# Five seven-product groups instead of three in FFN1, on eight single PSUM banks, with a new order of steps

## The chip, the cores and the metric

The kernel runs on one core of a Trainium2 chip. Times are device microseconds (us) of that core; "span" is the time from the first to the last instruction in a profiled execution, 1.7 to 2.4 us less than the timed value. Engines: PE is the matrix engine (TensorE), PEld its weight load, DVE VectorE, ACT ScalarE, POOL GpSimd, SP SyncE. PSUM is where the kernel has PE put its products, in eight banks; its other tiles lie in SBUF.

## The reference

```python
scores = np.matmul(q, k.transpose(0, 1, 3, 2)) / np.sqrt(64)   # q, k, v: (8, 8, 576, 64)
scores = np.where(np.abs(pos[:, None] - pos[None, :]) <= 32, scores, -1e9)
x = softmax(scores) @ v                       # -> tokens: (4608, 512)
g, val = x @ w_gate, x @ w_val                # w: (512, 1536)       "FFN1"
out = (g * sigmoid(g) * val) @ w_out          # w_out: (1536, 512)   "FFN2"
```

## The kernel before

The 4608 tokens are nine chunks of 512. Attention for the next chunk is woven into FFN2 of the present one. From chunk 1 on, products of 2 x 2 blocks are done with seven block products instead of eight (a Winograd form of Strassen's scheme), which costs sums of blocks on DVE and POOL. In FFN1 three groups use it; six hidden tiles are plain "units". FFN2 uses it for everything.

```python
PSUM: ps_a 2 double banks, ps_c 1 double bank, ps_o 2 single banks, open for the whole kernel

def ffn1_grouped(j):
    load_v(j + 1, range(5))                      # POOL's DMA queue
    xs = x_sums(j, nc.gpsimd)                    # four sums of xT, 128x512, on POOL (DVE in chunk 1)
    ...                                          # carried pairs: AV, norm, DMA transpose x -> xT
    # (cut) three groups of P1..P7, six units, q/k loads q0..k4 on POOL's queue between them
    # FFN2 sums: As = wino_sums(j, 0, 1, nc.gpsimd), Ds = wino_sums(j, 1, 2, nc.gpsimd),
    #            Bs = wino_sums(j, 2, 5)         # DVE, three groups wide: 128x768

def wino_sums(j, lo, hi, eng=None):
    tt = lambda o, a, b, op: (eng or nc.vector).tensor_tensor(out=o, in0=a, in1=b, op=op)
    return [lambda: tt(s1, a21, a22, ALU.add), lambda: tt(s2, s1, a11, ALU.subtract),
            lambda: tt(s3, a11, a21, ALU.subtract), lambda: tt(s4, a12, s2, ALU.subtract)]

def pair_xt(m):  nc.sync.dma_start_transpose(out=dst, in_=x16[0])      # x -> xT, SP's queue
def pair_mask(m): nc.vector.tensor_tensor(out=flat, in0=flat, in1=mask, op=ALU.mult)
```

Of the kernel before, what the change touches and what calls it, by code (L numbers as in the profile page):

```python
# [132 lines left out]
def kernel(  # L133
# [29 lines left out]
    qk16 = fast.enter_context(tc.tile_pool(name="qk16", bufs=4))  # L163
    tkpool = fast.enter_context(tc.tile_pool(name="tk", bufs=18))
# [6 lines left out]
    ps_a = fast.enter_context(tc.tile_pool(name="ps_a", bufs=2, space=bass.MemoryType.PSUM))  # L171
    ps_c = fast.enter_context(tc.tile_pool(name="ps_c", bufs=1, space=bass.MemoryType.PSUM))
    ps_o = fast.enter_context(tc.tile_pool(name="ps_o", bufs=2, space=bass.MemoryType.PSUM))
# [102 lines left out]

    def cast_qk(st, cast):
        t16 = qk16.tile([128, J9, 2, D], FP16, tag="qk16", name="t16")
        cast(t16.rearrange("p j h d -> p h j d"),
             st.rearrange("p h (j d) -> p h j d", d=D))  # L280
        return t16
# [56 lines left out]
    def quad_scores(ms, F):  # L338

        if ms not in quads:  # L340
            quads[ms] = ppool.tile([128, 2, 2, 2, HP, 64], FP16, tag="p2", name="p2_t", bufs=2)
            for n, m in enumerate(ms):
                pts[m] = quads[ms][:, n]
# [56 lines left out]
    def turn_x(ms, pool, cast=None):  # L400
# [15 lines left out]
        cast(dst.rearrange("p g (n t) -> p n g t", t=128), tp)  # L416
# [38 lines left out]
    def group_weights():  # L455

        s3 = qkst.tile([128, 3, 2, 768], FP16, tag="qkst", name="g_top")
        s4 = const.tile([128, 2, 768], FP16, name="g_rest")
        half = lambda w, k: w[:, 2 * k:2 * k + 2].rearrange(
            "p k (a c) -> p k a c", c=512)[:, :, :, 0:256]  # L460
        v0, v1, g0, g1 = half(wv16, 0), half(wv16, 1), half(wg16, 0), half(wg16, 1)
        gw["s"] = [s3[:, 0], s3[:, 1], s3[:, 2], s4]
        t1, t2, t3, t4 = [t.rearrange("p k (a c) -> p k a c", c=256) for t in gw["s"]]
        return [lambda k=k, o=o, a=a, b=b, op=op:
                nc.vector.tensor_tensor(out=o[:, k], in0=a[:, k], in1=b[:, k], op=op)
                for o, a, b, op in ((t1, g0, g1, ALU.add), (t2, t1, v0, ALU.subtract),
                                    (t3, v0, g0, ALU.subtract), (t4, v1, t2, ALU.subtract))
                for k in range(2)]

    def group_steps(j, i, xs, tiles):  # L470

        f = 2 * i
        x = xts[j]
        b11, b21, b22 = x[:, 0:2, 0:256], x[:, 2:4, 0:256], x[:, 2:4, 256:512]
        wv = lambda k: wv16[:, 2 * k:2 * k + 2, 512 * i:512 * i + 256]
        wg = lambda k: wg16[:, 2 * k:2 * k + 2, 512 * i:512 * i + 256]
        s1, s2, s3, s4 = [t[:, :, 256 * i:256 * i + 256] for t in gw["s"]]
        k = {}
        first = "ZX" if i == 2 else "X"

        def product(name, lhs, rhs, first):
            for n in range(2):
                for g in range(2):
                    nc.tensor.matmul(out=k[name][:, n], lhsT=lhs[:, g, 128 * n:128 * n + 128],  # L484
                                     rhs=rhs[:, g, :], start=(first and n == 0 and g == 0),
                                     stop=(g == 1), skip_group_check=True)

        def bank(name):
            pool = tiles[name]
            t = pool.tile([128, 2, 256], FP32, tag="c" if pool is ps_c else "o",  # L490
                          name=f"g{name}_ps")
            k[name] = t

        def keep_act(name, src):
            k[name] = opool.tile([128, 2, 256], FP32, tag="kept", name="kept", bufs=3)
            cast_act(k[name], k[src])

        def val(c, src, name):
            if "val" not in k:
                k["val"] = qk16.tile([128, 2, 512], FP16, tag="qk16", name="val")  # L500
            nc.vector.tensor_tensor(out=k["val"][:, :, 256 * c:256 * c + 256], in0=k[src],  # L501
                                    in1=k[name], op=ALU.add)
# [5 lines left out]
        def silu(c, src):  # L508
            if "silu" not in k:
                k["silu"] = qk16.tile([128, 2, 512], FP16, tag="qk16", name="silu")  # L510
            nc.scalar.activation(out=k["silu"][:, :, 256 * c:256 * c + 256], in_=k[src],  # L511
                                 func=AF.Silu, bias=0.0, scale=1.0)

        return {
            "P1": lambda: ([bank(n) for n in first], product("X", wv(0), b11, True)),
            "s1": lambda: keep_act("s1", "X"),
            "P2": lambda: (bank("Y"), product("Y", wv(1), b21, True)),
            "c11": lambda: val(0, "Y", "s1"),
            "P5": lambda: ("Z" in k or bank("Z"), product("Z", s1, xs[0], True)),
            "p5": lambda: keep_act("p5", "Z"),  # L520
            "P6": lambda: product("X", s2, xs[1], False),
            "u2": lambda: keep_act("u2", "X"),
            "P7": lambda: product("X", s3, xs[2], False),
            "c22": gate,
            "sc": lambda: silu(1, "gate"),
            "P3": lambda: product("Z", s4, b22, False),
            "c12": lambda: val(1, "Z", "u2"),
            "P4": lambda: product("X", wg(1), xs[3], False),
            "sd": lambda: silu(0, "X"),
            "hm": lambda: nc.vector.tensor_tensor(out=hts[j][:, 2 * f:2 * f + 2, :],  # L530
                                                  in0=k["silu"], in1=k["val"], op=ALU.mult),
        }

    def x_sums(j, eng):

        x = xts[j]
        b11, b12 = x[:, 0:2, 0:256], x[:, 0:2, 256:512]
        b21, b22 = x[:, 2:4, 0:256], x[:, 2:4, 256:512]
        t = ppool.tile([128, 4, 2, 256], FP16, tag="p2", name="x_sums", bufs=2)
        t1, t2, t3, t4 = [t[:, n] for n in range(4)]  # L540
        for o, a, b in ((t1, b12, b11), (t2, b22, t1), (t3, b22, b12), (t4, b21, t2)):
            eng.tensor_tensor(out=o, in0=a, in1=b, op=ALU.subtract)  # L542
        return t1, t2, t3, t4

    def unit_steps(j, fk):
# [3 lines left out]
        def half(i, w, parts=None):  # L549
            if i == 0:  # L550
                k["gv"] = ps_a.tile([128, 2, 512], FP32, tag="a", name="gv_ps")
            for g, c in parts or [(g, slice(0, 512)) for g in range(GS)]:
                nc.tensor.matmul(out=k["gv"][:, i, c], lhsT=w[:, g, 128 * fk:128 * fk + 128],  # L553
                                 rhs=xts[j][:, g, c], start=(g == 0 and c.start == 0),
                                 stop=(g == GS - 1), skip_group_check=True)

        def silu():
            k["s"] = spool.tile([128, 512], FP16, tag="s", name="ssb")
            nc.scalar.activation(out=k["s"], in_=k["gv"][:, 0, :], func=AF.Silu, bias=0.0,  # L559
                                 scale=1.0)  # L560

        first, second = [(0, slice(0, 256))], [(0, slice(256, 512))]
        most = [(g, slice(0, 512)) for g in range(1, GS)]
        return {"pg": lambda: half(0, wg16), "pv": lambda: half(1, wv16), "s": silu,
                "pva": lambda: half(1, wv16, first), "pvb": lambda: half(1, wv16, second),
                "pvm": lambda: half(1, wv16, most), "pvn": lambda: half(1, wv16, most + second),
                "m": lambda: nc.vector.tensor_tensor(out=hts[j][:, fk, :], in0=k["s"],  # L567
                                                     in1=k["gv"][:, 1, :], op=ALU.mult)}
# [3 lines left out]
    def wino_weights():  # L572
# [3 lines left out]
        rest = qkst.tile([128, 2, FKS // 2, 256], FP16, tag="qkst", name="ws_rest")  # L576
# [12 lines left out]
    def wino_sums(j, lo, hi, eng=None):  # L589

        h = hts[j].rearrange("p (f c) q -> p f c q", c=2)[:, lo:hi]
        a11, a21 = h[:, :, 0, 0:256], h[:, :, 0, 256:512]
        a12, a22 = h[:, :, 1, 0:256], h[:, :, 1, 256:512]
        s1, s2, s3, s4 = [t[:, lo:hi] for t in ws["s"]]
        tt = lambda o, a, b, op: (eng or nc.vector).tensor_tensor(out=o, in0=a, in1=b, op=op)  # L595
        return [lambda: tt(s1, a21, a22, ALU.add), lambda: tt(s2, s1, a11, ALU.subtract),
                lambda: tt(s3, a11, a21, ALU.subtract), lambda: tt(s4, a12, s2, ALU.subtract)]

    def wino_steps(j, split):
# [24 lines left out]
        def product(dst, lhs, rhs, first):  # L624
            for n in range(2):
                for f in range(FKS // 2):
                    nc.tensor.matmul(out=dst[n], lhsT=lhs[:, f, 128 * n:128 * n + 128],  # L627
                                     rhs=rhs[:, f, :],
                                     start=(first and f == 0 and (split or n == 0)),
                                     stop=(f == FKS // 2 - 1), skip_group_check=True)  # L630

        def keep_act(name, src):
            t = opool.tile([128, 2, 256], FP32, tag="kept", name="kept", bufs=3)
# [13 lines left out]
        def total(src, name, i, c, put=True):  # L647
# [13 lines left out]
            "p1": lambda: product(x, a(0, 0), b11, True),  # L661
            "s1": lambda: keep_act("s1", x),
            "p2": lambda: product(y, a(0, 1), b21, True),
            "c11": lambda: total(y, "s1", 0, 0),
            "p6": lambda: product(x, s2, t2, False),
            "u2": lambda: keep_act("u2", x),
# [326 lines left out]
```

## Time and profile before

| | before |
|---|---|
| time, median of 3 runs | 321.18 us (319.95 to 323.24) |
| span of the profiled run, granted clock | 317.8 us, 0.993 |
| chunks 1 to 8, start to start (the last to PE's end) | 32.07, 32.50, 32.00, 32.28, 31.77, 32.30, 29.30, 29.41 us |
| waits of PE with a named releaser after 59 us, summed | 0.6 us |

The prediction below reads the page, the stretches and PE's timeline (columns: start, time, engine, line, operation, tiles, how many, and in brackets the idle time before). In the timeline of VectorE in chunk 2's FFN2 (columns: start, time, engine, line, operation, tiles, how many, and in brackets the idle time before) a wide and a narrow sum together take 0.75 us, three masks 1.88 us.

```profile
113.17 0.75 DVE L595 TENSOR_TENSOR s_top<-hT 128x768 f16<-128x768 f16 x2
...
115.68 1.88 DVE L322 TENSOR_TENSOR p_t<-p_t,mask 128x1024 f16<-128x1024 f16 x3
```

POOL's timeline of the same place: it has only DMA issues there, until the new chunk's token sums. Those wait for xT, and stand in the queue in front of the q/k loads (tok).

```profile
110.78 2.67 POOL L242 DMA_DIRECT2D v<-in_v_dram  x3
...
123.15 1.53 POOL L542 TENSOR_TENSOR x_sums<-xT 128x512 f16<-128x512 f16 x1 [4.12 <-DVE xT L271]
...
128.08 0.92 POOL L223 DMA_DIRECT2D tok<-in_q_dram  x1
```

### The profile page before, as it was taken

The numbers are of one execution on the slowest core, as the hardware profiler recorded it, in microseconds if no ns is written. First come the engines' busy times: TensorE is split into PE (matmuls) and PEld (weight loads), VectorE is DVE, ScalarE is ACT, GpSimd is POOL, SyncE is SP. The second block draws the span as 40 slices with busy tenths as digits, with TensorE's granted clock in tenths as the row PEclk, the third lists the DMA queues.
The fourth block names the chain that finished last, engine by engine and source line by source line (L and its number), as shares of the span: only waits on it lengthen the run. The fifth ranks groups of instructions, "written<-read, shape, count | busy, mean of one in ns | idle before, by whom it ended". The sixth has DMA issues, their size and how long they took to land.

```text
span 317.8 us, 8145 instructions
## 1 busy us (share of the span) xinstructions
PE 303.6 (96%) x3220; PEld 213.2 (67%) x3220; DVE 219.1 (69%) x404; ACT 192.7 (61%) x309; POOL 182.4 (57%) x231
## 2 busy tenths in 40 slices
PE   5779999999999999999999999999999999999991
PEld 3444555676877687768776877677767776777581
DVE  2654398788866787678757885887588958737760
ACT  3774559665756575667466846684668566336530
POOL 8973678649358934994489339953440538303300
PEclk9999999999999999999999999999999999999997
DMA  7999999999959996999799989999651330030012
GB/s 274 166 192 296 244 179 177 200 143 165 158 136 128 172 163 142 121 183 152 164 132 161 159 171 124 136 175 163 153 127 42 95 92 3 24 110 0 0 51 92
DMA packets 155916, 44.22 MB, mean 139 GB/s; under 512 B 136416, under 2 KB 153312, under 8 KB 155872
## 3 DMA queue, kind: packets, MB, share of 16 engines
q0 software_dynamic: 100640, 16.52, 79.3%
q1 hardware_dynamic: 55232, 27.11, 40.7%
q8 instruction: 27, 0.44, 0.6%
q14 instruction: 17, 0.14, 0.2%
HBM read 37.75 MB, written 9.44 MB: 148 GB/s over the span
## 4 chain that ended last, share of the span: by engine, by line
PE 88%; DVE 4%; DMA 3%; ACT 2%; issue 1%; SPq 0%; ACTq 0%
PE gv_ps L553 26%; PE gX_ps L484 13%; PE x_ps L627 12%; PE y_ps L627 9%; PE gZ_ps L484 7%; PE gv_ps L427 6%; PE o_ps L374 4%; PE gY_ps L484 3%; PE ob L441 3%; PE s_ps L312 3%; DMA qk_st<-in_k_dram 3%; PE xt_ps L414 1%; DVE s_top L595 1%; PE z_ps L627 1%; DVE p_t L358 1%
## 5 line engine op out<-in xcount | busy, mean ns | idle before, releaser
L553 PE MATMUL gv_ps<-xT,wv 128*128 128x512 f16 (+1 forms) x224 | 57.2, 349 | 0.0
L553 PE MATMUL gv_ps<-xT,wg 128*128 128x512 f16 x192 | 49.4, 379 | 0.0
L542 POOL TENSOR_TENSOR x_sums<-xT 128x512 f16<-128x512 f16 x14 | 17.4, 1246 | 49.1 <-DVE xT L271 29.3
L595 POOL TENSOR_TENSOR s_top<-hT 128x256 f16<-128x256 f16 x32 | 21.6, 674 | 40.1 <-PE gY_ps L484 28.8
L318 ACT ACTIVATE p_t<-s_ps 128x1024 f16<-128x1024 f32 (+1 forms) x40 | 34.7, 924 | 14.2 <-PE s_ps L312 14.2
L268 ACT ACTIVATE kept<-gX_ps 128x512 f32<-128x512 f32 x48 | 28.6, 595 | 18.1 <-PE gX_ps L484 18.1
L567 DVE TENSOR_TENSOR hT<-ssb,gv_ps 128x512 f16<-128x512 f16 x48 | 32.7, 682 | 9.9 <-ACT ssb L559 9.9
L559 ACT ACTIVATE ssb<-gv_ps 128x512 f16<-128x512 f32 x48 | 28.6, 596 | 17.1 <-PE gv_ps L553 17.1
L506 DVE TENSOR_TENSOR gate<-gX_ps,kept 128x512 f32<-128x512 f32 x24 | 16.6, 692 | 25.9 <-PE gX_ps L484 17.0
L553 PEld LDWEIGHTS <-wv 128*128 128x128 f16 x224 | 21.9, 98 | 17.9
L484 PEld LDWEIGHTS <-g_top 128*128 128x128 f16 x288 | 27.5, 98 | 6.6 <-ACT kept L268 1.5
L627 PEld LDWEIGHTS <-hT 128*128 128x128 f16 x288 | 27.4, 98 | 5.3 <-issue 0.3
L627 PEld LDWEIGHTS <-s_top 128*128 128x128 f16 x288 | 27.7, 98 | 4.1 <-issue 0.6
L511 ACT ACTIVATE silu<-gate 128x512 f16<-128x512 f32 x24 | 15.1, 630 | 24.5 <-DVE gate L506 24.5
L484 PE MATMUL gX_ps<-x_sums,g_top 128*128 128x256 f16 x192 | 28.8, 273 | 0.0
L553 PEld LDWEIGHTS <-wg 128*128 128x128 f16 x192 | 17.6, 98 | 14.6
L501 DVE TENSOR_TENSOR val<-gY_ps,kept 128x512 f16<-128x512 f32 x24 | 16.5, 687 | 14.8 <-ACT kept L268 13.6
L223 POOL DMA_DIRECT2D tok<-in_q_dram x30 | 25.8, 860 | 1.1 <-DMA wo<-in_moe_w_out_dram 1.1
L223 POOL DMA_DIRECT2D tok<-in_k_dram x30 | 25.9, 862 | 0.5 <-DMA wo<-in_moe_w_out_dram 0.5
L392 DVE TENSOR_TENSOR x<-o_ps,rall 128x512 f16<-128x512 f32 x36 | 24.9, 691 | 1.2
L627 PE MATMUL x_ps<-w_top,s_top 128*128 128x256 f16 x192 | 23.6, 273 | 0.0
L322 DVE TENSOR_TENSOR p_t<-p_t,mask 128x1024 f16<-128x1024 f16 x32 | 21.4, 705 | 1.8 <-ACT p_t L318 1.1
(114 smaller groups left out, 618.4 us busy)
## 6 DMA issues: line engine op xcount, KB each, us to landing
out_dram<-osb SPq DMA_DIRECT2D x32, 256.0 KB, 3.1
v<-v SPq DMA_DIRECT2D x12, 264.0 KB, 5.7
v<-in_v_dram POOLq DMA_DIRECT2D x24, 128.0 KB, 7.1
tok<-in_q_dram POOLq DMA_DIRECT2D x24, 128.0 KB, 6.3
tok<-in_k_dram POOLq DMA_DIRECT2D x24, 128.0 KB, 6.5
qk_st<-in_q_dram SPq DMA_DIRECT2D x4, 576.0 KB, 6.9
qk_st<-in_k_dram SPq DMA_DIRECT2D x4, 576.0 KB, 9.1
v<-in_v_dram POOLq DMA_DIRECT2D x16, 96.0 KB, 6.7
```

Of the source, the lines that this page charges most:

```text
L223: nc.gpsimd.dma_start(out=t[0:n].rearrange("p (h d) -> p h d", d=D), in_=src[b].rearrange("h s d -> s h d")[128 * m:128 * m + n])
L268: nc.scalar.activation(out=o, in_=i, func=AF.Copy, bias=0.0, scale=1.0)
L318: nc.scalar.activation(out=o, in_=s, func=AF.Exp, bias=0.0, scale=1.0 / float(D) ** 0.5)
L322: nc.vector.tensor_tensor(out=flat, in0=flat, in1=mask, op=ALU.mult)
L392: nc.vector.tensor_tensor(out=x16s[m][:, a], in0=ov[:, :, :, 0:D], in1=r.unsqueeze(3).to_broadcast([128, a.stop - a.start, 4, D]), op=ALU. ...
L427: nc.tensor.matmul(out=gv[:, i, :], lhsT=w[:, g, 128 * fk:128 * fk + 128], rhs=xts[j][:, g, :], start=(g == 0), stop=(g == GS - 1))
L484: nc.tensor.matmul(out=k[name][:, n], lhsT=lhs[:, g, 128 * n:128 * n + 128], rhs=rhs[:, g, :], start=(first and n == 0 and g == 0), stop=( ...
L553: nc.tensor.matmul(out=k["gv"][:, i, c], lhsT=w[:, g, 128 * fk:128 * fk + 128], rhs=xts[j][:, g, c], start=(g == 0 and c.start == 0), stop ...
L559: nc.scalar.activation(out=k["s"], in_=k["gv"][:, 0, :], func=AF.Silu, bias=0.0, scale=1.0)
L567: "m": lambda: nc.vector.tensor_tensor(out=hts[j][:, fk, :], in0=k["s"], in1=k["gv"][:, 1, :], op=ALU.mult)}
L595: tt = lambda o, a, b, op: (eng or nc.vector).tensor_tensor(out=o, in0=a, in1=b, op=op)
L627: nc.tensor.matmul(out=dst[n], lhsT=lhs[:, f, 128 * n:128 * n + 128], rhs=rhs[:, f, :], start=(first and f == 0 and (split or n == 0)), st ...
```

## The change

Its intent: five of six hidden-tile pairs go through the seven-product scheme instead of three, so FFN1 needs fewer matmul columns. To interleave five groups, PSUM is closed and reopened as eight single banks for FFN1 and as the old pools for FFN2. The order of all steps is written out anew, with a bank behind `@` and an engine behind `/` (D is DVE, G is POOL). FFN2's sums are single 256-wide instructions now, 24 a chunk, spread over DVE and POOL, partly within FFN2.

```diff
+    def open_psum(*pools):
+        psum.close()
+        return [psum.enter_context(tc.tile_pool(name=n, bufs=b, space=bass.MemoryType.PSUM,
+                                                reuse_waits="tile")) for n, b in pools]
 ... (cut: chunk 0 builds the weight sums of five groups, 16 instructions, from unit 4 on)
-    def wino_sums(j, lo, hi, eng=None):          # one sum over several groups
+    def wino_sum(j, p, n, eng):                  # one sum of one group p
 ...
-    ORDER = """ pg0 pva0 pvm0 q0 k0 q1 t0 1P1 1s1 ... """
+        "even": """ (start and FFN1 cut) ... 4sd 4h0 u51m
+            4h1 S30/D tabE S40/D sc0@4@5 sc12@0@1@2@3 S50/D S51/D S02/G S41/D F1a@6 ex0 ex2 ld3 F1
+            S01/D Fs1 F2@7 S12/G S10/G k2 S11/G ex1 S31/G k0 F6 k1 S52/G Fc11 S33/D av012@4@5@0@1@2@3
+            S22/D m1 S42/G m0 F5 Fu2 F7 S13/G Fk5 sc34@4@5@0@1 m2 ex4 xtp@2@3 S43/D ex3 S53/D S03/G
+            Fc22 tabS xtc/D k4 F3 F4 Fc12 Fc21 k3 """
+        for token in ORDER[name].split():
+            if stage == 0 and banks and step[:3] != "av" and step[:3] != "u50":
+                single = open_psum(*[(f"ps_{i}", 1) for i in range(8)])
+            elif stage == 1 and step in ("sc0", "sc12", "F1a"):
+                ps_a, ps_c, ps_o = open_psum(*PAIRED)
```

In that order S30 is the first sum of group 3, F6 the FFN2 product that reads all sums S·1 (which are built from S·0), k a softmax mask, m a normalisation, av012 the attention products of three pairs, T1 to T4 the token sums. A carried pair is an attention pair left over from the chunk before.

## The prediction

> **What bounds the kernel now.** I read the page first: the busy shares and the chain of work that ended last.
>
> ```profile
> PE 303.6 (96%) x3220; PEld 213.2 (67%) x3220; DVE 219.1 (69%) x404; ACT 192.7 (61%) x309; POOL 182.4 (57%) x231
> ...
> PE 88%; DVE 4%; DMA 3%; ACT 2%; issue 1%; SPq 0%; ACTq 0%
> ```
>
> The matrix engine carries 88% of the chain. I then cut the span at the first matmul of each chunk and asked for busy time by stretch; four of the stretches are these (chunks 1, 3, 7, 8).
>
> ```profile
> 59.70:91.78 32.08, 32.08 (x359) 23.74 (x358) 27.34 (x52) 20.53 (x34) 16.42 (x22) 1.00 1.70 151
> ...
> 124.28:156.29 32.01, 32.01 (x358) 23.70 (x358) 23.95 (x44) 20.22 (x34) 22.41 (x28) 1.00 1.58 148
> ...
> 252.64:282.04 29.40, 28.98 (x222) 21.37 (x222) 19.04 (x34) 13.53 (x25) 13.27 (x15) 1.00 0.18 54
> 282.04:317.80 35.76, 29.20 (x222) 21.13 (x220) 18.60 (x38) 15.29 (x30) 5.51 (x8) 0.94 0.14 47
> ```
>
> Columns are the stretch, its length, then busy time of PE, weight load, DVE, ACT and POOL, granted clock, DMA. PE is busy for the whole of chunks 1 and 3; only chunks 7 and 8 (0.4 us, and the 6 us tail) show idle time. Busy is not the same as at peak, so I looked at start-to-start times in PE's timeline of chunk 3.
>
> ```profile
> 130.20 0.60 PE L484 MATMUL gX_ps<-x_sums,wg 128*128 128x256 f16 x4
> 130.63 0.60 PE L484 MATMUL gX_ps<-xT,wv 128*128 128x256 f16 x4
> 131.07 0.27 PE L553 MATMUL gv_ps<-xT,wv 128*128 128x256 f16 x1
> ...
> 142.04 1.03 PE L553 MATMUL gv_ps<-xT,wg 128*128 128x512 f16 x4
> 142.91 1.03 PE L553 MATMUL gv_ps<-xT,wv 128*128 128x512 f16 x4
> 143.77 1.47 PE L627 MATMUL x_ps<-wo,hT 128*128 128x256 f16 x12
> ```
>
> Four 256-column matmuls take 0.437 us (130.20 to 131.07 is eight), so 109.3 ns each; eight 512-column ones take 1.73 us, so 216 ns each. These leave no slack: FFN1 of a chunk is a packed stream of columns, and only fewer columns or fewer matmuls make it shorter.
>
> **What the Trainium skill says.** "TensorE: Matmul & The Clock Gate", section "Wait — 56ns, not 53.3ns?", gives N/2.4 GHz plus about 2.5 ns start to start, 109.2 and 215.8 ns here: the trace agrees (109.3, 216). The same page, "What's actually happening", says an idle window of about 3.4 us halves PE's clock until a busy window has passed; before has no such gap in its middle and a clock of 1.00 there, so this case does not show it yet. "SBUF — State Buffer", "Who interferes with whom", says a DVE instruction with two SBUF inputs and a GpSimd instruction that reads SBUF exclude each other. The trace fits: the DVE product of silu and val (both SBUF) averages 822 ns in chunk 3 and 682 in chunk 1, where POOL meets it less. "PSUM — Partial Sum Buffer", "PSUM bank collisions raise a hardware error", says two engines must not be in one bank at once. So product P6, which adds into the bank that s1 is copied from, has to wait for ACT; the trace shows the weight load of such a product waiting 0.21 us for the copy in chunk 8.
>
> **The change part by part.** *Matmul columns.* Before, FFN1 of a chunk has three groups of 7 x 4 = 84 matmuls of 256 columns and six plain units: 42 matmuls of 512 columns and six split ones, 12 of 256. That is 96 x 109.3 + 42 x 216 ns = 10.49 + 9.07 = 19.57 us (trace, 124.28 to 143.93: 19.65). After, five groups are 140 matmuls of 256 and two units 16 of 512: 15.30 + 3.46 = 18.76 us. Saved: 0.81 us a chunk, **6.5 us** over eight. FFN2 keeps 84 matmuls, only reordered (F1a does ten of the first twelve, so it can start before the last pair). Scores, AV and transposes keep their number.
>
> *Evictions.* A group costs more outside PE. Spacing of back-to-back instructions in chunk 8's timeline gives the real price:
>
> ```profile
> 285.17 0.60 ACT L268 ACTIVATE kept<-gZ_ps 128x512 f32<-128x512 f32 x1 [0.39 <-PE gZ_ps L484]
> ...
> 285.67 0.59 ACT L268 ACTIVATE kept<-gX_ps 128x512 f32<-128x512 f32 x1
> ...
> 287.02 0.69 DVE L506 TENSOR_TENSOR gate<-gX_ps,kept 128x512 f32<-128x512 f32 x1
> ...
> 287.62 0.68 DVE L501 TENSOR_TENSOR val<-gZ_ps,kept 128x512 f16<-128x512 f32 x1
> ```
>
> 0.50 us for an ACT copy, 0.60 for a DVE op from PSUM. Narrow f16 sums on DVE start 0.21 apart, one of 512 elements about 0.34, a softmax normalisation 0.75. DVE in the new FFN1: ten val and five gate 9.0, products 4 x 0.60 + 2 x 0.33 = 3.1, two unit products 1.2, four token sums 1.4, early FFN2 sums 0.6, carried norms 0.8 to 1.5: about 16.4 of 18.8 us, 87%. Before: nine 5.4, three 1.8, six 3.6, sums about 2.3, norm 0.8: 13.9 of 19.65, 71%. ACT: 15 copies 7.5, ten silu 5.2, two unit silu 1.0: 13.7, 73%. A group asks DVE for 2.4 us and ACT for 2.5 while PE spends 3.06 on it, so neither becomes the bound on average, and the interleaving over eight banks puts two or three other products (0.9 to 1.3 us) between P1 and P6, about what a copy and its hand-over need. I allow **+1.0 us** in all for small bank waits, collisions with POOL's 12 to 15 sums a chunk, and the two reopenings of the pools, and take off **0.3** for the gaps in chunks 7 and 8.
>
> *Chunk 0.* Here I expect most of the saving to go. The group weights are now computed from unit 4 on instead of unit 8, in 16 DVE instructions instead of 8. The top one takes the fourth slot of the four-buffer staging pool; its last tenant is the fourth q/k tile of batch 1, free only when POOL has cast it. POOL's timeline, then DVE's, then PE's:
>
> ```profile
> 33.91 1.15 POOL L274 CAST t<-qk_st 128x1152 f16<-128x1152 f32 x1 [1.44 <-DMA qk_st<-in_q_dram]
> 36.53 1.15 POOL L274 CAST t<-qk_st 128x1152 f16<-128x1152 f32 x1 [1.48 <-DMA qk_st<-in_k_dram]
> ```
>
> ```profile
> 31.30 0.69 DVE L434 TENSOR_TENSOR hT<-ssb,gv_ps 128x512 f16<-128x512 f16 x1 [1.04 <-ACT ssb L433]
> 33.52 0.69 DVE L434 TENSOR_TENSOR hT<-ssb,gv_ps 128x512 f16<-128x512 f16 x1 [1.54 <-ACT ssb L433]
> ...
> 39.81 1.02 DVE L465 TENSOR_TENSOR g_top<-wg 128x768 f16<-128x768 f16 x2
> ```
>
> ```profile
> 34.42 0.67 PE L287 MATMUL qk_ps<-ident,t 128*128 128x128 f16 x9
> 34.92 1.03 PE L427 MATMUL gv_ps<-xT,wg 128*128 128x512 f16 x4
> ```
>
> That cast waits for a DMA and ends at 36.53 + 1.15 = 37.68. Before, the first group sum came at 39.81, after it. Now it stands right behind unit 4's product (31.30), so DVE, in order, is blocked from 32.0 to 37.7. Then two sums (1.0) and unit 5's product (0.69) run to about 39.5. PE has two double-bank buffers for units: unit 6 still goes, unit 7 (34.92 before) must wait for unit 5's buffer, so PE starts again near 39.5. That is **+4.6 us**, and nothing behind it has slack to take it back, since PE is packed to the end of chunk 7. A 4.6 us idle gap is longer than the skill's 3.4 us window; a whole free-running window falls inside with chance (4.6 - 3.4) / 3.4, about a third (an estimate from that page), costing some 1.7 to 3 us: **+0.7** on average.
>
> Sum: 321.2 - 6.5 - 0.3 + 1.0 + 4.6 + 0.7 = 320.7.
>
> **The rivals.** (1) *The clean saving*: the staging slot is free in time or the wait is not drawn. Then 321.2 - 6.5 - 0.3 + 1.0 = 315.4, 1.8% faster. For it: whoever chose unit 4 may have looked at the result. Against it: the DMA-bound cast at 36.5, which nothing in the change moves earlier. I give it 15%. (2) *DVE becomes the bound in FFN1*: with 87% average load and in-order waits on ACT, POOL and PE, bank releases come late and PE stalls 0.5 to 1 us a chunk, 4 to 8 us in all: 324 to 327 with the chunk 0 stall. For it: POOL lengthens DVE's products, and DVE carries two more groups. Against it: eight banks let PE run two to three groups ahead, and DVE has over 2 us of slack a chunk; 12%. (3) *DMA*: the mean busy share is in the nineties until 230 us, so chunks shorter by 2.5% could meet late q/k loads. Against: a load lands 6.5 us after issue and is needed a chunk later. I count nothing for it.
>
> **Range and chances.** Weighing the main case (320.7) against rival 1 below it and rival 2 above it, I put 320.0, with 315.8 to 323.0 for 8 in 10. Over 2% faster (below 314.8) needs rival 1 and hardly any bank wait: 0.06. Over 2% slower (above 327.6) needs rival 2 at its worst and the clock loss: 0.03. Within 2%: 0.91.
>
> **What would show it.** Right: chunk 0's PE timeline has a gap of 4 to 5 us before unit 7, released by DVE, and DVE's first group sum starts at about 37.7 after waiting for POOL's cast; chunks 1 to 6 are 31.2 to 31.6 us long; FFN1's matmuls keep 109.3 and 216 ns. Wrong: no such gap and chunks 1 to 6 below 31.4 us (rival 1); chunks still at 32 us or more with PE waiting on DVE's val, gate or sums (rival 2); a granted clock below 1 between 39 and 46 us would price the throttle.

## More of the kernel before

POOL does its eight sums of FFN2 (two of six groups) while FFN1 runs; FFN2 itself has none of its sums on POOL.

The view of the tile xT between 110 and 138 us gives, from issue to landing of its DMA transposes:

```profile
DMA to landing us min/median/max: 2.4/2.6/3.2
```

## The result, and the profile after

The changed kernel takes 350.25 us in the median of four runs (347.86 to 353.17) against 321.28 us (319.95 to 323.24) of the kernel before. The ratio is 1.087, with a 95% interval of 1.077 to 1.098: slower, and outside the predicted range. Ratios here are the mean time of one kernel's runs over that of the other's of the same rounds, so not quite the ratio of the medians. Executions over 1.5% slower than the fastest of the same kernel are left out of the means.

On the page, PE's busy time is what it was (303.6 us before), but its share of the span has fallen from 96% to 88%. The chain of work breaks off after 2% of the span in this trace, so it couldn't be used; the stretches and the timeline took its place.

```profile
PE 304.5 (88%) x3380; PEld 230.9 (67%) x3380; DVE 266.8 (77%) x497; ACT 217.0 (63%) x357; POOL 190.8 (55%) x250
...
PE 2%; DVE 0%; ACT 0%; issue 0%
```

The stretches of chunks 2 (up to its last FFN2 matmul, with the wait in front) and 3:

```profile
92.60:130.70 38.10, 33.74 (x394) 26.37 (x392) 29.86 (x56) 24.19 (x39) 25.36 (x32) 0.96 1.37 131
134.12:167.19 33.07, 31.87 (x392) 26.17 (x393) 28.94 (x54) 23.01 (x38) 19.36 (x25) 1.00 1.12 131
```

Before, PE was busy for all of chunk 3; now 1.2 us of it are idle, and 4.4 us of the chunk 2 stretch, where the clock is 0.96 too. PE's timeline says what it waits for. The lines are, in turn: unit 7 of chunk 0; FFN1 of chunk 1; an attention product in chunk 1's FFN2; the start of chunk 2 (three lines); product F6 in chunk 2; the starts of chunks 3 and 4.

```profile
34.44 1.03 PE L441 MATMUL gv_ps<-xT,wg 128*128 128x512 f16 x4
...
61.26 0.60 PE L509 MATMUL gZ_ps<-x_sums,g_top 128*128 128x256 f16 x4
61.70 0.60 PE L509 MATMUL gY_ps<-xT,wv 128*128 128x256 f16 x4
...
85.20 0.96 PE L385 MATMUL o_ps<-v,p_t 128*64 128x66 f16 x48 [1.70 <-DVE p_t L331]
...
95.34 1.03 PE L583 MATMUL gv_ps<-xT,wv 128*128 128x512 f16 x2 [2.57 <-DMA xT<-x]
96.17 1.91 PE L583 MATMUL gv_ps<-xT,wg 128*128 128x512 f16 x4
97.88 0.79 PE L583 MATMUL gv_ps<-xT,wv 128*128 128x512 f16 x2
...
121.33 1.49 PE L654 MATMUL x_ps<-w_top,s_top 128*128 128x256 f16 x12 [1.43 <-DVE s_top L624]
...
134.12 1.02 PE L583 MATMUL gv_ps<-xT,wv 128*128 128x512 f16 x4 [3.34 <-DMA xT<-x]
...
171.10 1.03 PE L509 MATMUL gX_ps<-xT,wv 128*128 128x256 f16 x8 [1.65 <-DVE hT L594]
```

FFN1 is as dense as predicted: groups of four matmuls start 0.44 us apart (61.26 and 61.70). The rest of the view is three kinds of wait. Summed over chunks 1 to 8 (start to start, less the plain time of the matmuls between, only where the trace names a releaser):

| PE waits for | where | sum |
|---|---|---|
| a late DVE result (sums, masks, hT, output sums) | FFN2 of all chunks | 16.5 us |
| the DMA transpose x to xT | start of chunks 2, 3, 5: 2.73, 3.50, 3.32 | 9.6 us |
| a PSUM bank at the reopening | start of chunks 4, 5, 6, 8: 1.71, 1.07, 1.69, 1.63 | 6.1 us |
| ACT | chunk 8 | 0.5 us |

That is 32.6 us (before rounding) against 0.6 us before. With the 6.5 us of saved columns, a start of chunk 1 that is 1.0 us earlier, and two spells of slow clock of 1.5 us each (behind the wait at 95 us eight matmuls take 3.25 us from 95.34 to 98.59, 1.73 at 216 ns; behind a wait of 2.44 us in chunk 7 24 matmuls take 4.09 us from 303.42 to 307.51, 2.62 at 109.3 ns), the balance is 32.6 - 0.6 - 6.5 - 1.0 + 3.0 = 27.5 us. The spans differ by 346.2 - 317.8 = 28.4 us. The 0.9 us left are small gaps without a releaser; some are matmuls whose records are missing.

Why two waits slowed the clock and others, longer ones, did not can be read from the stretches. In each trace the changes of clock lie on a grid of 3.41 us. Four stretches of that grid in after (PE's busy time stands behind the comma, the clock third from the end):

```profile
91.43:94.84 3.41, 1.34 (x13) 0.95 (x10) 1.29 (x2) 1.33 (x3) 0.00 (x0) 1.00 2.55 114
94.84:98.25 3.41, 2.91 (x7) 1.03 (x8) 0.85 (x2) 0.00 (x0) 1.84 (x2) 0.50 1.42 261
...
128.97:132.39 3.42, 1.81 (x17) 1.37 (x15) 1.81 (x3) 2.58 (x4) 2.84 (x4) 1.00 2.41 142
132.39:135.80 3.41, 1.68 (x24) 0.81 (x25) 0.42 (x1) 0.00 (x0) 0.00 (x0) 1.00 2.01 197
```

Of the first PE was busy for 1.34 us, and the second ran at half clock. The wait of 3.34 us is cut in two by the boundary at 132.39, PE was busy for 1.81 and 1.68 us of the two stretches, and the clock stayed full.

Two timelines, of DVE and of POOL, show where the late results come from (the first line of each is chunk 0's, used further down):

```profile
31.42 1.44 DVE L483 TENSOR_TENSOR g_top<-wg 128x768 f16<-128x768 f16 x2
...
118.07 1.18 DVE L624 TENSOR_TENSOR s_top<-hT 128x256 f16<-128x256 f16 x3
119.28 1.99 DVE L624 TENSOR_TENSOR s_top<-s_top,hT 128x256 f16<-128x256 f16 x3
121.20 2.35 DVE L331 TENSOR_TENSOR p_t<-p_t,mask 128x1024 f16<-128x1024 f16 x3
```

```profile
36.06 1.47 POOL L280 CAST t<-qk_st 128x1152 f16<-128x1152 f32 x1 [1.48 <-DVE hT L448]
...
119.06 1.40 POOL L624 TENSOR_TENSOR s_top<-hT 128x256 f16<-128x256 f16 x2
120.42 0.71 POOL L624 TENSOR_TENSOR ws_rest<-hT,s_top 128x256 f16<-128x256 f16 x1
...
123.14 2.65 POOL L248 DMA_DIRECT2D v<-in_v_dram  x3
...
126.53 0.91 POOL L229 DMA_DIRECT2D tok<-in_q_dram  x1
```

Three sums of 256 columns take 1.99 us where they need about 0.28 each, and all of that time POOL is adding too. From the start and end times in the trace: of DVE's 87 FFN2 sums, 31 are over 60 ns longer than the shortest of their form, and all 31 overlap a POOL sum; so do all ten lengthened masks of 32 and all 17 lengthened hT products. All 31 sums end 0.14 to 0.16 us after a POOL sum that was running when they started; eleven more meet a POOL sum, but start before it or just before its end, and are not lengthened. Over the whole kernel the excess of DVE's TENSOR_TENSOR instructions over the shortest of their line and form is 30.7 us, 7.2 us before. Instructions with an input in PSUM show none (0 of 120 of the val and gate sums are over 60 ns).

The POOL timeline has the second thing as well: the v loads, at 110 us before, go out from 122 us, and the token loads follow at once. The transpose is issued into them, as SP's queue and the view of tile xT show:

```profile
126.26 1.67 SPq L419 DMA_TRANSPOSE xT<-x  x1
```

```profile
DMA to landing us min/median/max: 4.7/6.2/7.7
```

### The profile page after: what moved, and what is told of

Same layout as the page of the kernel before. It is cut to its first block, busy times and chain, and to the rows that moved or that the text cites. A ratio compares the mean times of both kernels' runs of the same rounds, so it can differ in the third digit from the quotient of the medians.

```text
span 346.2 us, 8664 instructions
## 1 busy us (share of the span) xinstructions
PE 304.5 (88%) x3380; PEld 230.9 (67%) x3380; DVE 266.8 (77%) x497; ACT 217.0 (63%) x357; POOL 190.8 (55%) x250
## 5 line engine op out<-in xcount | busy, mean ns | idle before, releaser
L624 POOL TENSOR_TENSOR s_top<-hT 128x256 f16<-128x256 f16 x60 | 42.1, 711 | 106.5 <-DVE hT L535 98.1
L274 ACT ACTIVATE kept<-gX_ps 128x512 f32<-128x512 f32 x80 | 46.4, 597 | 16.3 <-PE gX_ps L509 14.2
L535 DVE TENSOR_TENSOR hT<-silu,val 128x1024 f16<-128x1024 f16 (+1 forms) x48 | 34.4, 720 | 2.5 <-ACT silu L531 0.8
L521 DVE TENSOR_TENSOR val<-gY_ps,kept 128x512 f16<-128x512 f32 x40 | 27.1, 683 | 10.1 <-PE gY_ps L509 7.8
L526 DVE TENSOR_TENSOR gate<-gX_ps,kept 128x512 f32<-128x512 f32 x40 | 27.4, 687 | 5.4 <-PE gX_ps L509 4.1
L521 DVE TENSOR_TENSOR val<-gZ_ps,kept 128x512 f16<-128x512 f32 x40 | 27.0, 681 | 1.4 <-PE gZ_ps L509 1.2
L509 PEld LDWEIGHTS <-g_more 128*128 128x128 f16 x256 | 25.1, 98 | 3.5
L509 PE MATMUL gX_ps<-xT,wv 128*128 128x256 f16 x160 | 22.5, 272 | 4.7 <-DVE hT L594 4.7
L583 PE MATMUL gv_ps<-xT,wv 128*128 128x512 f16 x64 | 17.9, 390 | 9.1 <-DMA xT<-x 9.1
L531 ACT ACTIVATE silu<-gX_ps 128x512 f16<-128x512 f32 x40 | 23.8, 596 | 2.6 <-PE gX_ps L509 2.4
```

What stands on the lines that cost most here:

```text
L274: nc.scalar.activation(out=o, in_=i, func=AF.Copy, bias=0.0, scale=1.0)
L509: nc.tensor.matmul(out=k[name][:, n], lhsT=lhs[:, g, 128 * n:128 * n + 128], rhs=rhs[:, g, :], start=(pool is not None and n == 0 and g == 0),
L521: nc.vector.tensor_tensor(out=k["val"][:, :, cols(c)], in0=k[src], in1=k[name], op=ALU.add)
L526: nc.vector.tensor_tensor(out=k["gate"], in0=k["X"], in1=k["p5"], op=ALU.add)
L531: nc.scalar.activation(out=k["silu"][:, :, cols(c)], in_=k[src], func=AF.Silu, bias=0.0, scale=1.0)
L535: nc.vector.tensor_tensor(out=hts[j][:, 2 * f:2 * f + 2, c], in0=k["silu"][:, :, c], in1=k["val"][:, :, c], op=ALU.mult)
```

## The experiments

The theory at the outset: the 28 us are three separate losses. (A) In chunks 4 to 8 the bank numbers don't match where the unit u50 lies. (B) POOL's sums in FFN2 hold up the loads, which then delay xT. (C) POOL's sums in FFN2 block DVE's. The main rival: DVE and POOL have too much work in FFN2, wherever it stands, or the seven-product groups themselves cost what they save. Each run was timed over three rounds unless said otherwise; before in the same rounds had a median of 320.3 to 321.3 us.

| run | edit | median us | ratio to before, 95% interval |
|---|---|---|---|
| after | the change | 350.25 | 1.087 [1.077, 1.098] |
| e1_banks | bank numbers | 346.57 | 1.081 [1.074, 1.088] |
| e2_gated | T1 on POOL, v loads behind it | 354.64 | 1.107 [1.100, 1.115] |
| e2b_tok | T1 on POOL, v loads in front | 348.47 | 1.084 [1.077, 1.091] |
| e3_dve | all FFN2 sums on DVE | 341.45 | 1.064 [1.059, 1.070] |
| e4_memset | POOL writes only (wrong result) | 327.46, one run | none |
| e5_three | e1 + e2b + e3 | 335.72 | 1.047 [1.039, 1.054] |
| e6_turns | e5 + q/k transposes first | 329.28 | 1.023 [1.016, 1.030] |
| e7_early_pool | e6, POOL keeps its FFN1 sums | 321.67 | 1.003 [0.998, 1.008] |
| e8_order | e7 + order of sums | 320.41 | 1.001 [0.997, 1.004] |
| e9_late_check | e8 + two more places | 318.75 | 0.995 [0.991, 0.998] |

### e1_banks: the bank numbers alone

```diff
-                steps[step](single[int(banks[0])])
+                steps[step](single[SWAP.get(j, (0, 1, 2, 3, 4, 5, 6, 7))[int(banks[0])]])
+    SWAP = {4: (2, 3, 0, 1, 4, 5, 6, 7), ... the same for 5, 6, 7, 8}
```

In the allocation of the built kernel, u50's double bank is banks 2 and 3 in chunks 1 to 3 but 0 and 1 in chunks 4 to 8. The order gives banks 0 and 1 to the first group's products.

> Alone: in chunks 4 to 8 the bank numbers of the interleaved groups are permuted (0 with 2, 1 with 3), so that the first group's product does not open in a bank under the first unit's double bank. Theory banks: the 1.6 to 1.7 us that PE waits for the unit's product on DVE at the start of chunks 4, 6 and 8, and the 0.9 us wait for a normalisation in chunk 5, go; some 5 to 6 us less than the changed kernel (about 343 to 345 us). Rival: DVE is late anyway and another wait takes their place; less than 2 us of gain.

The start of chunk 4 in PE's timeline (171.10 above):

```profile
170.22 0.45 PE L385 MATMUL o_ps<-v,p_t 128*64 128x66 f16 x16
170.60 1.05 PE L509 MATMUL gX_ps<-xT,wv 128*128 128x256 f16 x8
```

The first group follows the attention product without a wait; the four waits are gone, and the span is 339.9 us against 346.2. Two of its four timed runs were slow, and the timed gain (1.087 to 1.081) is smaller than the spread of either kernel, so part A is shown by the trace and not resolved by the timing alone. The waits for xT (2.75, 3.60, 3.15) and for DVE stay.

### e2_gated and e2b_tok: what delays xT

```diff
 e2_gated:
-        if 2 < b < B:
-            load_v(b, range(5))
 ...
+            if step == "T1":
+                steps[step](nc.gpsimd)          # waits for xT, and the queue behind it too
+                if 2 < b < B:
+                    load_v(b, range(5))
 e2b_tok: T1 on nc.gpsimd alone; the v loads stay in front
```

> Alone: the first token sum goes back to POOL and the v loads are issued behind it, so POOL issues no load of the next chunk before that chunk's xT has landed. Theory loads: the DMA transposes of x land late (5.6 to 7.7 us after issue, before 2.4 to 3.5) because POOL's loads run beside them; with the gate they land in about 3 us, the waits of 2.6, 3.3 and 3.2 us at the start of chunks 2, 3 and 5 shrink below 1 us, and the time falls by 7 to 11 us (339 to 343). Rival: the transposes are late because the normalisations before them are late; landing stays over 5 us or the waits stay over 2 us, and the time falls by less than 3 us.

The waits for xT at the chunk starts are gone. The view of tile xT from 120 to 128 us, for the transpose that chunk 3 starts with, in after and in e2_gated:

```profile
DMA to landing us min/median/max: 7.7/7.7/7.7
```

```profile
DMA to landing us min/median/max: 2.5/2.5/2.5
```

So they were late because of the loads beside them, and not because of late normalisations, which was the rival of the expectation. But the kernel is slower than after. PE's timeline of chunk 3 has a new wait in place of the old:

```profile
153.06 0.61 PE L321 MATMUL s_ps<-qT,kT 64*128 64x64 f16 x16 [1.22 <-DMA kT<-tok]
156.42 0.40 PE L321 MATMUL s_ps<-qT,kT 64*128 64x64 f16 x8 [2.75 <-DMA kT<-tok]
```

Everything behind the gate is late now: the v loads of chunk 3 are issued from 129.40 us, at the chunk's start, instead of 12 us ahead of it, the token loads behind them, and the q/k transposes on SP's queue go out one after another up to 154 us. The clock adds to it: in this trace it stands at half for 17.1 us before the tail, in after for 6.8 us.

> The changed kernel with only the first token sum of each chunk on POOL; the v loads stay in front of it, the token loads of the next batch fall behind it. Theory loads, refined: POOL's late FFN2 sums push the v loads into the end of the chunk, so the v loads alone still cross the DMA transposes of x: landing falls from 6 to 7 us to about 4 to 5, the waits at the start of chunks 2, 3 and 5 shrink by half at most, 1 to 4 us gained against the changed kernel. If the token loads alone were the cause, the waits go wholly, 7 to 9 us gained, and no wait for kT appears (the first gate made one by delaying the v loads, which the queue of the turns waits for).

With the v loads in front again the waits for xT are 2.12, 1.93 and 2.74 us, from 2.57, 3.34 and 3.16, and the time is within the spread of after. The transposes that chunks 2, 3 and 5 start with still land after 6.0, 6.3 and 5.8 to 7.0 us (6.5, 7.7 and 7.4 to 7.5 in after, 2.4 to 2.5 in e2_gated). So taking the token loads away helps little while the v loads stay. Part B is real, but it isn't cured by holding up a queue: what is held up is needed later.

### e3_dve and e4_memset: is it the work or the collision?

```diff
 e3_dve:
-                steps[step](engines[eng])
+                steps[step](nc.vector if step[0] == "S" else engines[eng])
 e4_memset (wrong result on purpose):
-        eng.tensor_tensor(out=o, in0=a, in1=b, op=op)
+        if eng is nc.gpsimd:
+            for _ in range(2):
+                eng.memset(o, 0.0)
+        else:
+            eng.tensor_tensor(out=o, in0=a, in1=b, op=op)
```

e3_dve gives DVE all 192 sums, 105 more than before the edit. e4_memset leaves POOL busy in the same steps of the order, but POOL only writes (and no longer waits for hT).

> Alone: the 12 to 15 FFN2 sums a chunk that stand on POOL go to DVE, order unchanged. Theory lock: POOL's sums block DVE's two-SBUF-input instructions (28 us of excess over their own minimum in all); without them the excess falls below 6 us, the waits of PE for s_top, for the masks and for hT in FFN2 mostly go, and the time falls by 10 to 20 us (330 to 340). Rival, DVE simply has too much work: 13 more sums a chunk at 0.21 us add 2.7 us of DVE work a chunk, PE waits more in FFN2, and the time stays or rises.

> Wrong result on purpose: each FFN2 sum on POOL is replaced by two memsets of the same output, so POOL stays busy with writes but reads no SBUF. Theory lock (through the shared read side): DVE's two-SBUF-input instructions fall back to their minimum (0.28 us for a sum, 0.68 for a mask), excess below 5 us, and the waits of PE for s_top and the masks shrink. If POOL's writes block DVE too, the excess stays above 10 us. The time also changes because POOL no longer waits for hT, so it is not compared closely.

The groups of instructions, for the sums that read s_top and hT (busy time, mean ns, idle before), of after, e3_dve and e4_memset:

```profile
L624 DVE TENSOR_TENSOR s_top<-s_top,hT 128x256 f16<-128x256 f16 x29 | 14.2, 519 | 0.2
```

```profile
L624 DVE TENSOR_TENSOR s_top<-s_top,hT 128x256 f16<-128x256 f16 x48 | 12.6, 283 | 0.2
```

```profile
L628 DVE TENSOR_TENSOR s_top<-s_top,hT 128x256 f16<-128x256 f16 x29 | 7.3, 284 | 0.2
```

48 of these sums cost DVE less than 29 did next to POOL's. On the pages DVE is busy for 265.2 us in e3_dve and 266.8 in after, though it has 105 sums more: POOL's share of the sums had cost DVE about what it took off. This, and a kernel faster by 9 us, speaks against the rival. But the 9 us are the net of several changes: the waits for masks go and those for xT shrink, since POOL is free to issue its loads, while new waits for kT of 1.11, 1.79 and 3.06 us appear. And three things missed the expectation. The time is just outside 330 to 340 us; the excess of DVE falls from 30.7 to 10.2 us, not below 6 (before has 7.2); and PE is still idle for 4.3 us behind s_top, 5.0 in after.

In e4_memset the excess falls to 8.4 us, not below 5, with DVE's list of work unchanged: 21 of its 87 sums overlap a memset, and none is lengthened (two memsets take 0.63 us, a POOL sum of after 0.76). The same POOL steps, writing only, don't lengthen DVE's sums. PE's idle time behind late DVE results in FFN2 is 13.6 us in after, 7.0 in e3_dve and 2.0 in e4_memset. That is one run and a wrong result, so its 327.46 us is no timing to quote a ratio of; but its trace settles that it is POOL's reading and not its presence. In it the waits for xT (1.82, 2.33, 1.33) and for banks stay, as they should, while the waits on masks and s_top are nearly gone.

### e5_three and e6_turns: the parts together

```diff
 e6_turns, in chunk(), on top of e5_three:
-            if i == len(pairs) - 1 and b < B:
-                for m in range(5): turn_qk(b, m) ...     # behind the carried pairs' x -> xT
+        if b < B:
+            for m in range(5): turn_qk(b, m) ...         # at the start of the chunk
```

> Three remedies together: bank numbers permuted in chunks 4 to 8, all FFN2 sums on DVE, first token sum on POOL (v loads in front of it, now early since POOL has no sums). If the three causes are separate, their gains add: all-DVE gave about 10 us, the banks about 5, the landing of xT another 3: 329 to 333 us, with the waits for s_top under 1 us each and for xT under 0.5. If they hide one another, it stays above 335.

All waits for xT and banks are gone. The time is 335.72 us, above 335, where the expectation put the case that the causes hide one another: the loss fell from 8.7% to 4.7%, not to zero, because kT is late in chunks 3 and 5 (2.10 and 3.38 us), and F6 in chunk 7 waits 2.34 us for its sums.

> The same with the DMA turns of the next batch's q and k issued at the start of the chunk, ahead of the carried pairs' transposes. With all sums on DVE, PE waited 1.1, 1.8 and 3.1 us for kT in chunks 1, 3 and 5; theory: the queue's turns stand behind transposes that wait for a normalisation, so these waits go, 3 to 6 us less than e5_three (324 to 329). Rival: the turns wait for the token loads or the v loads themselves; then the waits stay and the time changes by less than 2 us.

On SP's queue the q/k transposes stood behind the carried pair's x transpose, which waits for normalised x, so for DVE. Put first, they are in time in chunks 3 and 5 (1.04 us stays in chunk 1). What remained in chunk 3 is this:

```profile
154.44 0.41 PE L385 MATMUL o_ps<-v,p_t 128*64 128x66 f16 x14 [2.22 <-issue]
```

PE waits 2.2 us in the middle of an attention product for nothing that the profile shows, and runs at half clock from 155.04 to 158.46 behind it. I found no cause of the wait; the run of the next section has the same DMA order and no such wait, so I leave it open.

### e7_early_pool: POOL adds only while FFN1 runs

```diff
-                steps[step](nc.vector if step[0] == "S" else engines[eng])
+                steps[step](nc.vector if step[0] == "S" and stage == 2 else engines[eng])
 and chunk 7's range check moved from FFN2 into FFN1
```

> The same as e6_turns, but the sums that POOL had during FFN1 stay on POOL (only those of FFN2 on DVE), and the range check of chunk 7 is moved from FFN2 into FFN1. Theory lock: in FFN1 most DVE work has one PSUM input and does not meet POOL, so the excess stays below 10 us while DVE has 4 to 8 sums a chunk less; the waits for s_top in FFN2 and the 2.3 us one in chunk 7 shrink: 1 to 4 us less than e6_turns, about 321 to 326. Rival: POOL's sums again push the v loads late and xT lands late; then it is slower than e6_turns.

321.67 us: the loss is gone, the gain not there. Of the 7.6 us to e6_turns, chunk 3 alone gives 4.0 in the traces (the unexplained wait and the slow clock after it) and chunk 0, which neither edit touches, 1.9 (in e6_turns it ran at half clock from 21.92 to 25.34); so only about 2 us are safely the placing of the sums. In chunk 2 F6 still waits after its first matmul, and so in chunks 4 and 6:

```profile
115.41 1.38 PE L654 MATMUL x_ps<-w_top,s_top 128*128 128x256 f16 x11 [0.56 <-DVE s_top L624]
```

### e8_order and e9_late_check: the remaining queue positions

```diff
 e8_order, even chunks: S10/G right after its product in FFN1, S01/D in FFN1; in FFN2
-  S50/D S51/D S02/G S41/D F1a@6 ... S01/D Fs1 F2@7 S12/G S10/G k2 S11/G ex1 S31/G k0 F6
+  S50/D S51/D S41/D F1a@6 ... S11/D S31/D Fs1 F2@7 k2 ex1 k0 F6         (S02, S12, S32 behind)
 e8_order, chunk 7: sums for F6 first, then those for F7 and F3
 e9_late_check, even chunks:
-  Fc11 S02/D S12/D av012@4@5@0@1@2@3 S22/D m1 S42/G m0 S32/D F5
+  Fc11 S02/D S12/D S22/D S32/D av012@4@5@0@1@2@3 m1 S42/G m0 F5
 e9_late_check: range check from FFN1 of chunk 7 to its end, its flag to the start of chunk 8
```

Both were timed over five rounds.

> The run with e7's edits plus a new order of the FFN2 sums, so that the ones that product F6 reads come first and the ones for F7 and F3 after it: in the even chunks the sums of group 1 are begun on POOL right after its product, in chunk 7 the sums for F6 are six on VectorE instead of eight mixed with others. Nothing else moves. The chunk lengths of e7 were 32.35, 32.35 and 32.35 us in the even chunks 2 to 6 (about 32.4 each) and 31.98 in chunk 7, with waits of 0.54 us in front of F6 in each even chunk and 0.48 and 0.93 us in chunk 7. Theory (the wait before F6 is only the position of these sums in the in-order queue of VectorE): those waits go, even chunks fall to 31.8 to 32.0, chunk 7 to 30.5 to 31.0, and the time is 318.5 to 320.5 us, ratio to before 0.992 to 0.999. Rival (VectorE is simply full in FFN2, so a sum taken away from one place is missed in another): the waits move to F7, F3 or the attention products, and the time stays at 321 to 322.5 us, ratio 1.000 to 1.005.

320.41 us and a ratio of 1.0006: the time lies within what the theory said, the ratio above it, where the rival is. The trace decides for the rival's mechanism in the even chunks: they stay at 32.34 us, and the wait moved from F6 to F7, whose fourth matmul stands 0.80 us for the sum S32. Chunk 7 fell from 31.98 to 31.34 us, not to 31.0, with a wait for a gate sum behind the range check:

```profile
269.65 0.60 PE L509 MATMUL gX_ps<-x_sums,wg 128*128 128x256 f16 x4 [0.72 <-DVE gate L526]
```

> The run with e8's edits plus two more places mended: in the even chunks the four sums that product F7 reads first stand ahead of the softmax normalisations m1 and m0 on VectorE (in e8's trace F7's fourth matmul waits 0.80 us for the one that stood behind m0), and chunk 7's range check, 2.0 us of VectorE in FFN1, goes to the end of chunk 7, its flag to the start of chunk 8 (in e8's trace a gate sum of 0.72 us and the hT product of 0.48 us are waited for behind it). Theory (these waits are the queue position of a few VectorE instructions): even chunks fall from 32.34 to 32.40 to about 31.6, chunk 7 from 31.34 to about 30.2, and the time to 317 to 319 us, ratio to before 0.988 to 0.997, which is then about half of the saved columns. Rival (the waits move to the attention products or to the next chunk's start): 320 us or more, ratio 0.998 to 1.003.

318.75 us, ratio 0.995 with an interval that ends below 1: as the theory said. But not by all of its steps. The gain is chunk 7's: 29.03 us, 31.34 in e8_order, of which chunk 8 gives 0.75 back (29.19 from 28.44). The even chunks stay at 32.33. Their wait moved once more, to an attention transpose that wants a normalisation (0.68 us in chunks 2 and 4) and to ws_rest in chunk 6 (1.28 us). Stretches of chunks 2 and 7:

```profile
91.01:123.34 32.33, 31.65 (x394) 26.06 (x392) 27.97 (x64) 24.44 (x40) 17.48 (x21) 1.00 1.81 151
...
251.63:280.67 29.04, 28.83 (x275) 23.92 (x273) 25.10 (x57) 16.93 (x31) 5.74 (x7) 1.00 0.16 48
```

DVE is busy 27.97 of 32.33 us in chunk 2, 87%. With this order the rival is right in its small form: in the even chunks DVE's FFN2 is full enough that a sum moved from one place is missed at another. e9_late_check is faster than both kernels, by 0.5% than before and by about 9% than after, and correct.

## Why the prediction was wrong, point by point

- **Columns: right.** FFN1 of chunk 2 takes 20.12 us from e7_early_pool on, with one attention product (0.38), three score products (0.81) and 0.19 for changing over between them, which the new order puts there: 18.7 us, as the 18.76 of the sum. The 6.5 us are really saved. One reading of before was wrong without harm: the trace has 44 matmuls of 512 columns in each FFN1 and eight halves, so four split matmuls and not six; that makes 92 x 109.3 + 44 x 216 ns = 19.56 us, and start to start it is 19.55.
- **FFN1 evictions: right.** DVE at 87% didn't bound FFN1; the trace of after has no wait for val, gate or kept in chunks 2 to 8 outside the reopenings. The worry of the second rival was in the wrong half of the chunk.
- **"I allow +1.0 us in all for small bank waits, collisions with POOL's 12 to 15 sums a chunk, and the two reopenings of the pools": the step that failed.** This term measured 16.5 us for late DVE results plus 6.1 us for banks. The mechanism stood in the prediction: two SBUF inputs on DVE and a POOL instruction that reads SBUF exclude each other. It was not applied to the place where the diff puts POOL's sums: inside FFN2, among DVE sums and masks which all have two SBUF inputs. Before, POOL did none there. e3_dve and e4_memset show this (of 13.6 us of idle PE behind late DVE results 2.0 stay when POOL only writes); e1_banks shows the banks. To bound it I would have had to count POOL's sums in FFN2, 6 to 10 a chunk and 69 in all: at 0.67 us each they could hold up DVE for 46 us (an estimate from the order and from the 0.67 us of before). Measured, DVE's excess without POOL's 105 sums is 20.5 us smaller (e3_dve).
- **"DMA ... I count nothing for it": the second step that failed.** 9.6 us of waits for xT appeared, and 1.5 us of slow clock behind one of them. The prediction looked at late q/k loads of before, which have a chunk's time, and not at the x transposes, which had about 5 us in chunk 2 of before (issued at 118.99, read at 124.22). There the order of POOL's queue kept other loads out of their way, and they landed in 2.4 to 3.2 us; the new order does not. e2_gated shows that the loads are the cause (2.4 to 2.5 us with none beside the transpose), and e2b_tok that the v loads in front suffice for most of the delay; no run moves the v loads alone.
- **The chunk 0 stall: did not occur.** "The top one takes the fourth slot of the four-buffer staging pool; its last tenant is the fourth q/k tile" was a guess at the allocator. In the built kernel g_top takes the slot of the first q/k tile. DVE's first group sums start at 31.42 us, 4.6 us before POOL's last cast at 36.06, and unit 7 starts at 34.44 without a wait. The +4.6 and +0.7 us fall away. Alone, that would have made the result 315.4, rival 1.
- **Clock.** The 0.7 us were tied to a stall that didn't come; the same loss came elsewhere, 1.5 us in chunk 2 and 1.5 us in chunk 7.

So where did the expected gain go? It was spent in FFN2 and at the chunk starts. With the three parts mended, e9_late_check is about 1.7 us faster than before (321.2 x 0.0054), but hardly any of that is the saving. Its chunk 1 starts 1.22 us earlier (58.42 against 59.64 us), and its chunks 1 to 8 together take 251.44 us, before's 251.64. Within the chunks the saving was spent on waits: from chunk 1 on PE is idle for 5.3 us behind results that the trace names, nearly all of DVE (0.7 to 1.3 us in each even chunk, and chunk 1 takes 32.59 us against 32.07); in before it is 0.5 us. Why DVE is late I put down to 24 narrow sums a chunk where before had wide ones. This I infer from DVE's busy time (27.97 us in chunk 2, 23.81 before); no run with wide sums was made.

## What to carry to other kernels

When a diff moves work between VectorE and GpSimd, look not at the loads of each but at which of their instructions will overlap: here sums with two SBUF inputs on both sides took turns as if on one engine, and the slower one set the price. Handing GpSimd sums that VectorE does in 0.28 us lengthened single sums of VectorE by up to 0.50 us, one by 0.96. And read an in-order queue as a schedule for everything behind its head: an instruction that waits may be what keeps later transfers out of the way of an urgent one.

## What the Trainium skill lacked or had wrong

- "SBUF — State Buffer", "Who interferes with whom": confirmed, and more sharply than I used it. All 31 lengthened DVE sums of after overlap a POOL sum; with POOL writing only (e4_memset) the same sums have their plain 284 ns, though 21 overlap a memset, as the page says of a GpSimd instruction that only writes. It lacks a price: here a 256-column sum went from 283 to 519 ns in the mean, and POOL's from 0.67 to 0.86 us for the form that reads ws_rest's inputs.
- "TensorE: Matmul & The Clock Gate", "What's actually happening": the halved clock fits exactly (four 512-column matmuls in 1.71 us from 96.17 to 97.88, 427 ns each), and so does a window of about 3.4 us: the clock changes on a grid of 3.41 us. But the window need not be idle throughout. A wait of 2.57 us at 95.34 brought the half clock, 2.07 us of it in one window, while 3.34 us at 134.12 and 3.16 us at 205.83, each cut by a boundary, did not (there four matmuls keep 0.87 us). In the twelve traces, from chunk 1 on, the clock fell after every full-clock window with 2.07 us or more of idle PE and after none with 1.93 or less; between them 1.97 brought it down and 2.05 did not. In chunk 0 one fall came after only 1.34 us, among small products and transposes (e6_turns, 21.92).
- No page that I read says how long a DMA transpose takes among other loads: between 110 and 138 us 2.4 to 3.2 us before, 4.7 to 7.7 us in after with the v and token loads in flight.
